# Letting GpSimd take some of VectorE's exponent shifts, in half tiles, in a planned transformer block

## The chip, the core and the metric

The kernel runs on one core of a Trainium2 chip. The engines that matter are TensorE (PE, matrix products), VectorE (DVE), ScalarE (ACT), GpSimd (POOL) and the DMA queue of SyncE (SP). Each engine works through its own list of instructions in order and waits on semaphores for the others. The metric is the device time of one execution in microseconds; the median of the runs shown is 819.32 us.

## The reference, cut to what matters

One transformer block with 2048 tokens of width 512, 32 heads of size 16, and a hidden width of 1376. Six modulation vectors come from a conditioning vector `c`.

```
h = layernorm(x) * (1 + ca) + sa
q, k, v = split(h @ wqkv)                   # 32 heads of 16
p = softmax(q k^T * 16**-0.5)               # 2048 x 2048 for each head
x = x + ga * ((p v) @ wo)
h = layernorm(x) * (1 + cb) + sb
x = x + gb * (gelu(h @ w1 + b1) @ w2 + b2)
```

The exponentials dominate: 32 heads of 2048 by 2048, over 134 million of them.

## The kernel before, in words

**Tiles.** Scores are held transposed, keys on partitions. Queries are cut into 4 blocks of 512 and heads into 8 groups of four, which makes 32 quads, `quads` (block, group). A quad has 16 key tiles of 128, and each key tile has 4 rows, one a head: a score row is a 128x512 product (`qk`, L1019). Four heads lie in four 32-row strips of the array.

**Two ways to an exponential.** Most key tiles go to ScalarE: `do_qk` puts units of 3 and 2 score rows in turn into PSUM tiles `sA` and `sB`, and `do_exp` (L1071) makes `pA` and `pB` with one ACTIVATE each. Four key tiles of a quad (`DKT`, in the first quad one) go through VectorE instead. `do_d` puts one score row at a time into one of two spare PSUM banks (`aux`). `do_pass` (L1137) adds a bias, clamps at zero and writes the number as int16 into a row of the tile `t0` (128x4x512). These 16 bits, read as float16, are roughly the wanted power of two. Three further copies, each `t0` plus a constant `MJ[j]`, are the same power scaled down by a fraction of a power of two; `do_shift` (L1155 to L1162, the instruction on L1158) makes each of them as one 128x2048 int16 instruction on VectorE, into a tile `t16`. There are 125 such tiles, so 500 passes and 375 shifts. Each of the four versions is multiplied with its own scaled copy of the values and all are summed, so that the mean of four rough powers approximates the exponential.

**Value products.** `do_pv` (L1190) multiplies a key tile, or one of its four versions, with the values and sums into one bank `od` for the quad. `do_out` (L1242) copies the sum to `o_sb` and sends the row sums through DRAM and back for the reciprocals (L1264); GpSimd then multiplies (`OT`, L1272). When all quads of a block are done, its output projection, MLP and result follow as jobs among the next block's quads (`tail_jobs`); the last block's come at the end (`last_tail`). A second way through the computation for extreme inputs (`general_path`) is not taken here.

**What sets the order.** While the program is built, a small planner steps a clock by 0.02 us (`DT`). At each step it asks the engines in turn, ACT, DVE, PE, POOL, SP (L1441), and the first thing that an engine finds ready is issued and booked with a price: `V_PASS` and `V_SHIFT` 0.61 us, an exponential 1.34 (three rows) or 0.92 (two), a GpSimd product 1.2 or 1.3. `run` (L960) moves that engine's `free` time; a result is seen by others 0.1 us (`SEM`) after its end. The chip then runs each engine's list in the planned order, held together by semaphores alone, not by the plan's times.

VectorE's step (`dve_step`, L1399) takes, in this order: a quad's `o_sb` copy, a job, a pass if a score row is ready, a shift. With more than four shifts pending a shift goes ahead of a pass. `shift_ready` (L1149) asks for a pending shift and a free `t16` (4 buffers). `shifts` gets its three entries when the last pass of a tile is issued (`do_pass`). `d_items` holds the score rows that were issued and not passed yet, two at most; `d_ready` (L1095) also asks for a free one of 3 `t0` tiles. GpSimd's step (`pool_step`, L1418) knows jobs alone: the `OT` products, eight weight scalings (`scale_wo`, L405) and twelve residual sums (L688). If more than one score tile of a quad is unstarted when the stream of ScalarE's rows runs dry, `fill_stream` (L992) gives one to ScalarE. `do_fill` (L1224) puts products with zeros into gaps of TensorE.

Of the kernel before, what the change touches and what calls it, by code (L numbers as in the profile page):

```python
# [11 lines left out]
ALU = mybir.AluOpType  # L12
# [3 lines left out]
I16 = mybir.dt.int16  # L16
# [4 lines left out]
P = 128  # L21
# [29 lines left out]
PE_, ACT_, DVE_, POOL_, SP_ = range(5)  # L51
# [22 lines left out]
V_PASS = 0.61  # L74
V_SHIFT = 0.61
V_EVAC = 0.63
TRIP = 5.0


# [8 lines left out]
MJ = [int(round(-math.log2(w) * STEP)) for w in WJ]  # L88
# [5 lines left out]
def adaln_block(ctx: ExitStack, tc: tile.TileContext, A_x, A_wqkv, A_wo, B_x, B_w1, B_b1, B_w2, B_b2,  # L94
                c, w_mod, out):
    nc = tc.nc
# [46 lines left out]
    def later_loads():  # L143
# [6 lines left out]
        for b in range(2, NQB):  # L150
# [19 lines left out]
                            op0=ALU.mult, op1=ALU.add)  # L170
# [41 lines left out]
    def ln_stats(src, st, t, i):  # L212
        nc.vector.bn_stats(out=st[:, i, :], in_=src[:, t, :])
# [101 lines left out]
    def q_proj(ps, ch, b, js=range(NC)):  # L315
        for j in js:
            nc.tensor.matmul(out=ps, lhsT=W_q[:, j, ch * P:(ch + 1) * P], rhs=hT[:, j, b * 512:(b + 1) * 512],  # L317
                             start=(j == 0), stop=(j == NC - 1))

    def q_evac(ps, ch, b, both=True):  # L320
        t = qmp.tile([P, 2, 512], BF16, name="qm")
        for par in range(2):
            if par and not both:
                nc.scalar.mul(out=t[:, par, :], in_=ps, mul=qmask[:, par:par + 1])
            else:
                nc.vector.tensor_scalar(out=t[:, par, :], in0=ps, scalar1=qmask[:, par:par + 1], scalar2=None,
                                        op0=ALU.mult)
        qm[(b, ch)] = t

    def v_proj(ps, kt, js=range(NC)):  # L330
        for j in js:
            nc.tensor.matmul(out=ps, lhsT=hT[:, j, kt * P:(kt + 1) * P], rhs=W_v[:, j, :],
                             start=(j == 0), stop=(j == NC - 1))

    def v_evac(ps, kt, eng="dve"):
        src = ps.rearrange("p (h d) -> p h d", d=16)
        dst = VE[:, kt, 0:H * HS].rearrange("p (h e) -> p h e", e=HS)[:, :, 0:16]
        if eng == "act":
            nc.scalar.copy(out=dst, in_=src)
        else:  # L340
            nc.vector.tensor_copy(out=dst, in_=src)
# [81 lines left out]
    tp = att.enter_context(tc.tile_pool(name="tp", bufs=T_BUFS))  # L423
# [16 lines left out]
    def job(at, rows, needs=(), label=None, hold=-1):  # L440
        jobs.append(Job(at, rows, needs, label, hold))
# [24 lines left out]

    def proj_job(at, mm, evac, needs, label, eng=DVE_, dur=V_EVAC):
        def f(part):
            def h(j):
                if part == 0:  # L470
                    j.ps = j.alloc()
                mm(j.ps, (0, 1) if part == 0 else (2, 3))
            return h

        def g(j):
            evac(j.ps)
        job(at, [(PE_, 2 * MM, f(0)), (PE_, 2 * MM, f(1)), (eng, dur, g)], needs, label, 2)

    def v_job(at, kt):
        eng = V_ENG[kt]  # L480
        proj_job(at, lambda ps, js: v_proj(ps, kt, js), lambda ps: v_evac(ps, kt, eng), [("h", kt // 4)], ("v", kt),
                 ACT_ if eng == "act" else DVE_, 0.5 if eng == "act" else V_EVAC)

# [3 lines left out]
    def q_job(at, ch, b, needs=()):  # L487
        proj_job(at, lambda ps, js: q_proj(ps, ch, b, js), lambda ps: q_evac(ps, ch, b), [("h", b), *needs],
                 ("q", ch, b), dur=2 * V_EVAC + 0.1)

# [12 lines left out]
    for b in range(1, NQB):  # L503
        at = 0.25 * (b - 1)
        def stats(j, b=b, t=0):
            if b > 1 and t == 0:
                st_of[b] = pron.tile([P, 12, 6], FP32, name="st1")
            ln_stats(xb[b], st_of[b], t, t)
        job(at - 0.16, [(DVE_, V_EVAC, lambda j, b=b, t=t, f=stats: f(j, b, t)) for t in range(ST1 if b == 1 else 0, 4)],
            [("n", b - 1)] if b > 1 else [], ("st", b))  # L510
# [81 lines left out]
    def tail_jobs(b):  # L592
# [15 lines left out]
        def oproj(tt):  # L608
            def f(part):
                def g(j):  # L610
                    if part == 0:
                        j.ps = j.alloc()
                        nc.tensor.matmul(out=j.ps, lhsT=ident, rhs=T["xr"][:, tt, :], start=True, stop=False)
                    for t in (2 * part, 2 * part + 1):
                        nc.tensor.matmul(out=j.ps, lhsT=OT[(b, t)][:, tt * P:(tt + 1) * P], rhs=W_o_pad[:, t, :],  # L615
                                         start=False, stop=(t == 7))
                return g
# [4 lines left out]
            def stats(j):  # L622
                ln_stats(T["x1"], T["st"], tt, tt)
            job(p0 + 0.5 + 0.25 * tt, [(PE_, (2 + (i == 0)) * MM, f(i)) for i in range(4)]
                + [(DVE_, V_EVAC, res), (DVE_, V_EVAC, stats)],
                [("begin", b)] + [("wo", t) for t in range(8)] + [("ot", b, t) for t in range(8)] + ([("o", b, tt - 2)] if tt > 1 else []),
# [20 lines left out]
        def up_(fc):  # L647
            def f(part):
                def h(j):
                    if part == 0:  # L650
                        j.ps = j.alloc()
                    for c in (2 * part, 2 * part + 1):
                        nc.tensor.matmul(out=j.ps, lhsT=late["W_1"][:, c, fc * P:(fc + 1) * P],  # L653
                                         rhs=T["h2"][:, c, :], start=(c == 0), stop=(c == NC - 1))
                return h

            def g(j):
                nc.vector.tensor_scalar(out=T["u"][:, fc, :], in0=j.ps, scalar1=late["b1c"][:, fc:fc + 1],  # L658
                                        scalar2=None, op0=ALU.add)
            job(p0 + 2.3 + 0.2 * fc, [(PE_, 2 * MM, f(0)), (PE_, 2 * MM, f(1)), (DVE_, V_EVAC + 0.05, g)],  # L660
                [("h2", b, c) for c in range(NC)], ("u", b, fc), 2)
# [283 lines left out]
    clock = 0.0  # L945
    free = [0.0, 0.0, 1.0, 0.0, 0.0]
# [6 lines left out]
    def seen_by(t):  # L953
        return t is not None and t + SEM <= clock
# [5 lines left out]
    def run(eng, dur, lat=0.08):  # L960

        free[eng] = clock + dur
        return clock + dur + lat

    def pe_run(dur, m):
        end = run(PE_, dur + (SWITCH if m != mode[0] else 0.0), PE_LAT)
        mode[0] = m
        pe_log.append((clock, dur))
        return end
# [119 lines left out]
    t0, t0_seq, t0_done = {}, [], {}  # L1089
    t_of, t_ready, shifts = {}, {}, deque()  # L1090
    t16_seq, pv_end = [], {}
    d_items, d_read = deque(), []
# [53 lines left out]

    d_prog = [0.0]

    def shift_ready():  # L1149
        if not shifts:  # L1150
            return False
        n = len(t16_seq)
        return n < T_BUFS or seen_by(pv_end.get(t16_seq[n - T_BUFS]))

    def do_shift():  # L1155
        qi, kt, j = shifts.popleft()
        t16 = tp.tile([P, 4, 512], I16, name="t16")
        nc.vector.tensor_scalar(out=t16, in0=t0[(qi, kt)], scalar1=float(MJ[j]), scalar2=None, op0=ALU.add)  # L1158
        end = run(DVE_, V_SHIFT)
        t16_seq.append((qi, kt, j))  # L1160
        t_of[(qi, kt, j)] = t16
        t_ready[(qi, kt, j)] = end  # L1162
        t0_done[((qi, kt), j)] = end


    od = {}
# [75 lines left out]
    def do_out(qi):  # L1242
# [27 lines left out]
        def mult(j):  # L1270
# [4 lines left out]
        needs = [("o", b - 1, tt) for tt in range(4)] if b and t else []  # L1275
        lab[("d", qi)] = end + TRIP
        jobs.insert(0, Job(-1.0, [(DVE_, 0.26, back), (SP_, TRIP, lambda j: None), (POOL_, 1.3, mult)],
                           [("d", qi), *needs], ("ot", b, t)))
# [12 lines left out]
    def start_ok(o, eng):  # L1291
        if o.at > progress() or o.rows[0][0] != eng or not all(has(x) for x in o.needs):
            return False
        if o.hold >= 0:
            if progress() > EARLY and any(a.hold >= 0 and a.i <= a.hold for a in active):
                return False
            return any(seen_by(t) for t in bank_rel)
        return True

    def job_for(eng):  # L1300

        best = None
        for o in active:
            if o.rows[o.i][0] == eng:
                same = o.i and o.rows[o.i - 1][0] == eng
                if (o.same if same else o.other) <= clock + 1e-6 and (best is None or o.at < best.at):
                    best = o
        for o in jobs[:24]:
            if best is not None and best.at <= o.at:
                break  # L1310
            if start_ok(o, eng):
                return o
        return best

    def do_job(o, eng):
        if o in jobs:
            jobs.remove(o)
            active.append(o)
            if o.hold >= 0:
                o.bank = next(i for i in range(len(banks)) if seen_by(bank_rel[i]))  # L1320
                bank_rel[o.bank] = INF
        e, dur, fn = o.rows[o.i]
        fn(o)
        if eng == PE_:
            end = pe_run(dur, "full")
            dur = free[PE_] - clock
        else:
            end = run(eng, dur)
        row_end(o, eng, dur, end)
# [86 lines left out]
        return False  # L1416

    def pool_step():  # L1418
        o = job_for(POOL_)
        if o is None:  # L1420
            return False
        do_job(o, POOL_)
        return True

    def sp_step():
        o = job_for(SP_)
# [60 lines left out]
```

## Time and profile before

| | |
|---|---|
| timed runs | 817.38, 819.32, 819.41 us; median 819.32 |
| the profiled execution | 815.8 us, span 814.0 us |
| granted TensorE clock | 0.996 |
| PE, DVE, ACT, POOL busy | 771.9, 723.8, 756.2, 71.2 us |
| passes (L1137) | 500, mean 682 ns |
| shifts (L1158) | 375, mean 715 ns, 629 to 1766 |
| exponentials pA, pB (L1071) | 310 and 309, mean 1513 and 1089 ns |
| GpSimd's OT products (L1272) | 31, mean 1394 ns |

How to read the profile: the page gives each engine's busy time, then the span in 40 slices with the busy tenths of each. A group's line is: source line, engine, operation, tiles written and read, shape, count, then busy us and mean ns of one, then the engine's idle time just before these instructions and what ended most of it. A timeline's line is: start and duration in us, engine, source line, operation, tiles, shape and count, and in brackets the idle time before; neighbours of a kind may be merged into one line. A windows line gives, for a stretch, the busy time of PE, PEld (weight loads), DVE, ACT and POOL with their counts, then the granted clock, the DMA share and GB/s. Durations of queued instructions overlap a little, so that the spacing of starts is the better measure of what one costs.

### The profile page before, as it was taken

The numbers are of one execution on the slowest core, as the hardware profiler recorded it, in microseconds if no ns is written. First come the engines' busy times: TensorE is split into PE (matmuls) and PEld (weight loads), VectorE is DVE, ScalarE is ACT, GpSimd is POOL, SyncE is SP. The second block draws the span as 40 slices with busy tenths as digits, with TensorE's granted clock in tenths as the row PEclk, the third lists the DMA queues.
The fourth block names the chain that finished last, engine by engine and source line by source line (L and its number), as shares of the span: only waits on it lengthen the run. The fifth ranks groups of instructions, "written<-read, shape, count | busy, mean of one in ns | idle before, by whom it ended". The sixth has DMA issues, their size and how long they took to land.

```text
span 814.0 us, 18164 instructions
## 1 busy us (share of the span) xinstructions
PE 771.9 (95%) x7404; PEld 237.5 (29%) x7470; DVE 723.8 (89%) x1306; ACT 756.2 (93%) x681; POOL 71.2 (9%) x62
## 2 busy tenths in 40 slices
PE   7999999989999999999999999999999999999997
PEld 3432222322223222222222322222222222222254
DVE  7879989999998998998998999988998999889663
ACT  4898999989998999999999999999999999999962
POOL 0000000024000000101100000011100000011100
PEclk9999999999999999999999999999999999999999
DMA  8100000104100000001100000010100000010100
GB/s 269 68 1 16 15 16 15 42 16 140 41 15 16 15 17 2 14 23 29 48 16 16 16 10 8 14 29 21 48 15 16 15 3 15 15 28 23 48 2 29
DMA packets 30426, 24.49 MB, mean 30 GB/s; under 512 B 13473, under 2 KB 24194, under 8 KB 30338
## 3 DMA queue, kind: packets, MB, share of 16 engines
q1 hardware_dynamic: 29650, 22.49, 9.6%
q8 instruction: 60, 0.98, 0.5%
q10 hardware_dynamic: 688, 0.79, 0.3%
q14 instruction: 28, 0.23, 0.1%
HBM read 20.65 MB, written 2.61 MB: 29 GB/s over the span
## 4 chain that ended last, share of the span: by engine, by line
PE 46%; ACT 24%; DVE 17%; issue 10%; DMA 2%; SPq 0%; POOL 0%; ACTq 0%; DVEq 0%; POOLq 0%
PE od L1214 14%; ACT pA L1071 14%; ACT pB L1071 9%; DVE t L1137 7%; PE sA L1019 6%; PE sB L1019 6%; DVE t L1158 6%; PE aux L1019 4%; PE aux L678 3%; PE od L1235 2%; PE aux L615 2%; PE aux L653 2%; PE aux L303 1%; PE fb L805 1%; PE aux L317 1%
## 5 line engine op out<-in xcount | busy, mean ns | idle before, releaser
L1071 ACT ACTIVATE pA<-sA 128x1536 bf16<-128x1536 f32 x310 | 469.1, 1513 | 16.3 <-PE od L1214 7.2
L1137 DVE TENSOR_SCALAR t<-aux 128x512 int16<-128x512 f32 x500 | 328.8, 682 | 30.6 <-PE aux L1019 29.2
L1071 ACT ACTIVATE pB<-sB 128x1024 bf16<-128x1024 f32 x309 | 336.4, 1089 | 6.3 <-PE od L1214 3.9
L1158 DVE TENSOR_SCALAR t<-t 128x2048 int16<-128x2048 int16 x375 | 260.1, 715 | 2.6 <-PE od L1214 1.4
L1019 PE MATMUL aux<-qm,kT 32*128 32x512 bf16 x500 | 177.5, 380 | 6.2 <-DVE t L1137 3.4
L1019 PEld LDWEIGHTS <-kT 32*128 32x128 bf16 x2048 | 75.9, 91 | 266.9 <-issue 262.6
L1214 PE MATMUL od<-pA,VE 128*32 128x512 bf16 x930 | 141.7, 385 | 0.6 <-DVE o_sb L1253 0.5
L1214 PE MATMUL od<-t,VV 128*32 128x512 f16 x1500 | 139.6, 385 | 1.5 <-DVE t L1158 1.2
L1214 PE MATMUL od<-pB,VE 128*32 128x512 bf16 x618 | 140.7, 385 | 0.1
L1019 PE MATMUL sA<-qm,kT 32*128 32x512 bf16 x930 | 123.0, 384 | 10.5 <-ACT pA L1071 4.7
L1019 PE MATMUL sB<-qm,kT 32*128 32x512 bf16 x618 | 121.1, 384 | 5.3 <-ACT pB L1071 2.4
L1272 POOL TENSOR_TENSOR OT<-o_sb,rb 128x512 bf16<-128x512 f32 x31 | 43.2, 1394 | 559.3 <-DMA rb<-d 288.4
L1214 PEld LDWEIGHTS <-VE 128*32 128x32 bf16 x2048 | 50.3, 94 | 95.9 <-issue 83.2
L1235 PE MATMUL od<-hT,zeros 128*32 128x512 bf16 x844 | 76.0, 385 | 0.0
L1214 PEld LDWEIGHTS <-VV 128*32 128x32 bf16 x1500 | 39.7, 95 | 58.8 <-issue 50.2
L1214 PE MATMUL od<-t,VE 128*32 128x512 f16 x500 | 49.5, 384 | 2.7 <-DVE o_sb L1253 2.7
L678 PE MATMUL aux<-W,uG 128*128 128x512 bf16 x120 | 35.5, 383 | 1.6 <-issue 1.6
L653 PE MATMUL aux<-h2T,W 128*128 128x512 bf16 x113 | 35.6, 384 | 0.5 <-issue 0.3
L1235 PEld LDWEIGHTS <-zeros 128*32 128x32 bf16 x872 | 21.8, 95 | 36.1 <-issue 30.6
L658 DVE TENSOR_SCALAR uG<-aux,b1c 128x512 bf16<-128x512 f32 x33 | 24.4, 741 | 4.8 <-PE aux L653 4.8
L615 PE MATMUL aux<-W_o_pad,OT 128*128 128x512 bf16 x88 | 25.6, 382 | 0.7 <-issue 0.5
L688 POOL TENSOR_TENSOR ob<-tmp,xr 128x512 bf16<-128x512 f32 x12 | 15.7, 1305 | 115.1 <-DVE tmp L684 115.1
(156 smaller groups left out, 430.9 us busy)
## 6 DMA issues: line engine op xcount, KB each, us to landing
rb<-d SPq DMA_DIRECT2D x124, 64.0 KB
W_m<-in_w_mod_dram SPq DMA_DIRECT2D x2, 1024.0 KB
xr<-in_A_x_dram SPq DMA_DIRECT2D x4, 512.0 KB
out_dram<-ob SPq DMA_DIRECT2D x15, 128.0 KB
xb<-in_A_x_dram SPq DMA_DIRECT2D x3, 512.0 KB
W<-in_B_w_dram SPq DMA_DIRECT2D x1, 1376.0 KB
W<-in_B_w_dram SPq DMA_DIRECT2D x1, 1280.0 KB
W_m<-in_w_mod_dram SPq DMA_DIRECT2D x1, 512.0 KB
```

Source lines behind the costliest of these rows:

```text
L615: nc.tensor.matmul(out=j.ps, lhsT=OT[(b, t)][:, tt * P:(tt + 1) * P], rhs=W_o_pad[:, t, :], start=False, stop=(t == 7))
L653: nc.tensor.matmul(out=j.ps, lhsT=late["W_1"][:, c, fc * P:(fc + 1) * P], rhs=T["h2"][:, c, :], start=(c == 0), stop=(c == NC - 1))
L658: nc.vector.tensor_scalar(out=T["u"][:, fc, :], in0=j.ps, scalar1=late["b1c"][:, fc:fc + 1], scalar2=None, op0=ALU.add)
L678: nc.tensor.matmul(out=j.ps, lhsT=T["u"][:, fc, tt * P:(tt + 1) * P], rhs=late["W_2"][:, fc, :], start=False, stop=(fc == NFC - 1))
L688: nc.gpsimd.tensor_tensor(out=o, in0=j.tmp, in1=T["x1"][:, tt, :], op=ALU.add)
L1019: nc.tensor.matmul(out=dst, lhsT=kT[32 * r:32 * r + 32, ch, kt * P:(kt + 1) * P], rhs=qm[(b, ch)][32 * r:32 * r + 32, par, :], start=True, ...
L1071: nc.scalar.activation(out=pt[:, 0:n, :], in_=st[:, 0:n, :], func=ACT.Exp, scale=math.log(2.0) / STEP)
L1137: nc.vector.tensor_scalar(out=t0[(qi, kt)][:, r, :], in0=sd, scalar1=T_BIAS, scalar2=0.0, op0=ALU.add, op1=ALU.max)
L1158: nc.vector.tensor_scalar(out=t16, in0=t0[(qi, kt)], scalar1=float(MJ[j]), scalar2=None, op0=ALU.add)
L1214: nc.tensor.matmul(out=od[qi][32 * r:32 * r + 32, :], lhsT=w, rhs=src, start=first, stop=last_)
L1235: nc.tensor.matmul(out=dst[32 * r:32 * r + 32, :], lhsT=zeros, rhs=hT[:, r, 0:512], start=bank is not None, stop=bank is not None)
L1272: nc.gpsimd.tensor_tensor(out=OT[(b, t)], in0=o, in1=j.rb, op=ALU.mult)
```

## The change

GpSimd may take a shift too, as two instructions over half of the tile each (two rows, 128x1024). A variable `port` in the planner holds the time up to which a shift, of either engine, is booked; no shift of either engine begins before that. It is not set by GpSimd's other work. GpSimd begins a shift when it has no job, a shift is ready, and at least one score row waits in `d_items`; the second half goes ahead of jobs, as soon as the booked time allows. A half is priced at 1.2 us. The shift's result counts as ready after the second half.

```diff
+P_SHIFT = 1.2
...
+    port = [0.0]
+    pool_cur = []
+
+    def shift_ready(eng=DVE_):
+        if not shifts or clock < port[0]:
             return False
...
         end = run(DVE_, V_SHIFT)
+        port[0] = free[DVE_]
...
+    def pool_shift():
+        if pool_cur:
+            key, t16 = pool_cur.pop()
+            part = 1
+        else:
+            key, part = shifts.popleft(), 0
+            t16 = tp.tile([P, 4, 512], I16, name="t16")
+            t16_seq.append(key)
+        qi, kt, j = key
+        nc.gpsimd.tensor_scalar(out=t16[:, 2 * part:2 * part + 2, :], in0=t0[(qi, kt)][:, 2 * part:2 * part + 2, :],
+                                scalar1=float(MJ[j]), scalar2=None, op0=ALU.add)
+        end = run(POOL_, P_SHIFT)
+        port[0] = free[POOL_]
+        if part == 0:
+            pool_cur.append((key, t16))
+        else:
+            t_of[key] = t16
+            t_ready[key] = end
+            t0_done[((qi, kt), j)] = end
...
     def pool_step():
+        if not pool_cur:
+            o = job_for(POOL_)
+            if o is not None:
+                do_job(o, POOL_)
+                return True
+        if pool_cur and clock >= port[0] or shift_ready(POOL_) and pool_may():
+            pool_shift()
+            return True
+        return False
+
+    def pool_may():
+
+        return len(d_items) >= 1
```

More of the change, by code (lines that the diff above doesn't have):

```diff
@@ L1147, in adaln_block @@
     d_prog = [0.0]
-    def shift_ready():
-        if not shifts:
+    port = [0.0]
+    pool_cur = []
+    def shift_ready(eng=DVE_):
+        if not shifts or clock < port[0]:
             return False
@@ L1418, in pool_step @@
     def pool_step():
[L1419 to L1423, printed above, removed]
+        if not pool_cur:
[9 more added lines that the diff above has]
+        return len(d_items) >= 1
     def sp_step():
```

## The prediction

> **What bounds the kernel now.** I read the page's busy lines first, to see which engines can matter.
>
> ```profile
> PE 771.9 (95%) x7404; PEld 237.5 (29%) x7470; DVE 723.8 (89%) x1306; ACT 756.2 (93%) x681; POOL 71.2 (9%) x62
> ## 2 busy tenths in 40 slices
> PE   7999999989999999999999999999999999999997
> ...
> DVE  7879989999998998998998999988998999889663
> ACT  4898999989998999999999999999999999999962
> ```
>
> Three engines are nearly full from about 60 to 770 us, and GpSimd is nearly empty. The groups say what each does:
>
> ```profile
> L1071 ACT ACTIVATE pA<-sA 128x1536 bf16<-128x1536 f32 x310 | 469.1, 1513 | 16.3 <-PE od L1214 7.2
> L1137 DVE TENSOR_SCALAR t<-aux 128x512 int16<-128x512 f32 x500 | 328.8, 682 | 30.6 <-PE aux L1019 29.2
> L1071 ACT ACTIVATE pB<-sB 128x1024 bf16<-128x1024 f32 x309 | 336.4, 1089 | 6.3 <-PE od L1214 3.9
> L1158 DVE TENSOR_SCALAR t<-t 128x2048 int16<-128x2048 int16 x375 | 260.1, 715 | 2.6 <-PE od L1214 1.4
> ```
>
> TensorE's 95% contains 844 filler multiplies (L1235). So the question is where ScalarE loses time, because its exponentials can't be shortened by this change. Its busy share hides that: a queued instruction is recorded as lasting longer than its pitch. I therefore took starts from ScalarE's timeline. Undisturbed, pA to pB is 1.33 us and pB to the next pA 0.91, so 2.24 a pair. Everything above that between the first and the last exponential adds up to **35.3 us**: 9.3 before 100 us, 1.1 from 100 to 150, 12.7 from 150 to 300, and 12.2 after that. No gain can pass this. The windows show why 150 to 300 is worst:
>
> ```profile
> 150.00:200.00 50.00, 46.84 (x508) 13.51 (x510) 48.45 (x83) 46.91 (x42) 11.46 (x13) 0.97 0.23 70
> 200.00:250.00 50.00, 47.39 (x452) 13.53 (x453) 46.88 (x75) 45.58 (x40) 5.63 (x4) 1.00 0.08 23
> 700.00:750.00 50.00, 48.05 (x468) 14.04 (x468) 43.50 (x72) 50.00 (x45) 6.74 (x5) 1.00 0.08 21
> ```
>
> The columns are PE, PEld, DVE, ACT, POOL. VectorE is at 48.45 of 50 where ScalarE falls to 46.91; late in the run VectorE has air (43.50) and ScalarE is full.
>
> One more view decides this case, the timeline around a GpSimd multiply:
>
> ```profile
> 583.21 1.27 POOL L1272 TENSOR_TENSOR OT<-o_sb,rb 128x512 bf16<-128x512 f32 x1 [11.10 <-DMA rb<-d]
> ...
> 583.34 1.69 DVE L1158 TENSOR_SCALAR t<-t 128x2048 int16<-128x2048 int16 x1
> ...
> 586.15 1.23 ACT L1071 ACTIVATE pB<-sB 128x1024 bf16<-128x1024 f32 x1
> ...
> 587.45 1.45 ACT L1071 ACTIVATE pA<-sA 128x1536 bf16<-128x1536 f32 x1
> ```
>
> A shift that starts under a GpSimd instruction doesn't slow down in proportion: it ends 0.55 us after GpSimd does (584.48 and 585.03), in 1.69 us where an undisturbed one takes 0.685. The passes (L1137, from PSUM) under the same multiplies keep their 0.68. The reverse holds too: that multiply, 1.27 us alone, lasts up to 1.84 behind a shift. So shifts and GpSimd exclude each other and passes do not. Here the delay of 1.0 us cost ScalarE 0.4: 1.30 from pB to pA in place of 0.91. I found eight shifts stretched by about 0.8 to 1.1 us and put ScalarE's next gaps beside them: 2.9 us after the two at 170 to 172, 1.9 after the two at 200 to 202, then 0.3, 0.9, 0.4, 0.6 after those at 213, 282, 583 and 606. That is 7.0 us, 0.9 a collision, 0.5 where VectorE has some air. Shorter ones (513, 650) cost nothing.
>
> **The change, part by part.**
>
> *How many shifts move.* GpSimd may take a shift when no shift runs and a score tile waits in a bank. In the trace a tile's three shifts are pending for 5.25 us on average (start of its last pass to start of its third shift); in 117 of 125 tiles there is a moment in that time when no shift runs and a score row has been issued but not passed. A moved shift holds the port 2.4 us by the plan's price, so two a tile is the ceiling. I take a little over one: 140 of 375, which is 280 half instructions.
>
> *Removed from VectorE.* 140 shifts at their start-to-start pitch of 0.60 (two in 1.28-1.29 us) are 84 us, 724 down to 640.
>
> *Added to GpSimd.* The trace has no one-input integer instruction on it. From below: a memset with no input, 0.205 us for 128x128 and 0.525 for 128x512, so 0.83 ns an element and 0.95 us for 1024. From above: the two-input product, 1.16 us undisturbed for 512, twice that for 1024, 2.3. The middle is about 1.6. I take 1.2, the plan's price, because the plan's other prices sit on the rows: 0.61 for a pitch of 0.60, 1.2 for a product of 1.16, 1.3 for one of 1.27, and one input lies nearer to the memset. GpSimd gains 280 x 1.2 = 336 us, 71 to 407, half the span, beside other work.
>
> The Trainium skill bears on this price from both sides: GPSIMD Engine Reference, "Engine selection", calls one-input work on GpSimd roughly line rate, while its section "Elementwise — side-by-side cycle accounting" gives about 1.8 cycles an element as the best of a tight loop. At the 1.2 GHz of that page, estimates are 0.85 us a half by the one, the forecast's side, and 1.5 by the other, where the first rival begins.
>
> *Queue order on GpSimd.* A half stands behind multiplies that wait for a DMA (L1272, 288 us of idle before it). The first ones start 4.9 to 5.2 us after the reciprocal; the plan allows 5.0 plus semaphores. Little is held up; at nothing. A multiply may wait for two halves, 2.4 us; the output projection that needs it comes quads later, so this costs nothing unless it is a group's last.
>
> *The wait that is new.* TensorE runs in order, so a value product waiting for a late t16 holds every score behind it. Today TensorE waits for shifts 1.2 us in all. From a shift's end to the first product on it the median is 1.3 us, but 120 of 375 have under 0.8. I charge 0.5 us.
>
> *The sum.*
> - Of the 7.0 us after collisions: fewer shifts are left (235 of 375) and they queue less, so half goes, -3.5.
> - Of the other 6.7 us lost from 150 to 300, where VectorE is full: half, -3.3.
> - Of the other 11.2 after 300, where it isn't: a tenth, -1.1.
> - Before 100 us shifts are few: 0.
> - New collisions: the order keeps halves and shifts apart on paper, but engines only keep to it through their semaphores. I allow 6 of 280 halves that stop a shift by 0.8 us or more, 0.5 each, +3.0.
> - Late t16: +0.5.
>
> Together -4.4 us. The profiled execution took 815.8 us (span 814.0 and 1.8 around it), so 811.4; the three timed runs have their median 3.5 higher, and from 819.3 I forecast **814.9 us**. A difference of 0.3% (2.5 us) is about what a measurement of this kernel can tell from no change.
>
> **The rivals.**
>
> *A, a half is dearer than its price* (slower). Every moved shift ends late by twice the excess, and the next shift on VectorE, placed right behind it, is stopped that long with all passes behind it. The relief is 0.60 a shift, so it decides from 1.2 + 0.30 = 1.5 us a half. At the middle, 1.58, 140 x (0.76 - 0.60) = 22 us, on a VectorE that is full in part of the run: some 17, or 836. At 2.2 it would be 140 x 1.4, near 200, or over 1000. For it: the product's 2.3 ns an element. Against: the memset's 0.83.
>
> *B, the exclusion costs more than the plan sees* (slower) though a half takes 1.2. The plan books a GpSimd half from the moment it places it; on the chip it starts when the last pass has written t0 and the shift in front has ended. In 69 tiles the chance falls inside the last pass, up to 0.69 us too early. If that shifts half of these so that the next shift is stopped for 0.8 us, at 0.5 each for 40, that is +20, less the gains of 7.9: +12, 831. For it: the rows at 583. Against: the passes run on, and VectorE has 84 us of relief. The Trainium skill says the same in Perfetto Trace Analysis, "Optimizing Scalar/DVE Operations": because the two share a port, moving work between them might not help.
>
> *C, nothing comes of it.* ScalarE is full after 300 us, and the gaps before are TensorE's, or GpSimd seldom finds a shift free. 819.
>
> **How the numbers follow.** Forecast 0.40, A 0.19, B 0.24, C 0.17. The forecast's own range is 806 (both losses from 150 to 300 and those after collisions gone, 13.7) to 817. The upper bound of the price lies far out in A; two in ten are left out by stopping at 840, which takes in B and the mild half of A. Faster by over 0.3%: the forecast less its weak end, 0.38. Within: C and that weak end, 0.19. Slower: A and B, 0.43.
>
> **What would show it.** Right: GpSimd halves near 1.2 us, some 280 of them; VectorE's busy time down by 60 to 90 us; few shifts over 1.4 us; ScalarE's gaps from 150 to 300 halved. A: halves of 1.5 us or more, and TensorE waiting for GpSimd by tens of us. B: halves of 1.2, but dozens of shifts over 1.4 us. C: all moved, ScalarE's gaps as before. I would also be wrong if score tiles of the exponent path went over to ScalarE (fewer than 500 passes).

## The result, and the profile after

The changed kernel takes **1147.69 us** (median of its runs, 1140.24 to 1155.53), the one before 818.35 in the same runs: **1.402 times as long, 95% interval 1.397 to 1.408**. The forecast of 814.9 and its whole range, up to 840, are missed by far. The profiled execution took 1143.97 us, with a span of 1141.9 in place of 814.0 and a granted clock of 0.825 in place of 0.996.

First the busy lines of the page, with the slices of GpSimd and of the granted clock:

```profile
PE 946.8 (83%) x7418; PEld 246.5 (22%) x7486; DVE 722.3 (63%) x1160; ACT 781.3 (68%) x681; POOL 905.7 (79%) x354
...
POOL 0069999889997986988997889957995977989820
PEclk9995886978769689798878888899679676688899
```

GpSimd went from 9% to 79%, and through most slices it stands at 7 to 9 tenths. The three engines that were nearly full are now at 63 to 83%. The windows view from 80 to 1080 us says it in microseconds (PE, PEld, DVE, ACT, POOL, clock, DMA share, GB/s):

```profile
80.00:1080.00 1000.00, 823.45 (x6461) 196.84 (x6516) 631.04 (x934) 688.10 (x573) 880.12 (x339) 0.80 0.06 16
```

GpSimd works for 880 of 1000 us: it is now the fullest engine. The groups show with what, and who waits:

```profile
L1181 POOL TENSOR_SCALAR t<-t 128x1024 int16<-128x1024 int16 x292 | 839.8, 2900 | 144.8 <-DVE t L1139 91.0
L1073 ACT ACTIVATE pA<-sA 128x1536 bf16<-128x1536 f32 x310 | 452.2, 1459 | 185.5 <-PE sA L1021 98.1
L1139 DVE TENSOR_SCALAR t<-aux 128x512 int16<-128x512 f32 x500 | 332.3, 684 | 302.1 <-PE aux L1021 249.5
L1241 PE MATMUL od<-t,VV 128*32 128x512 f16 x1500 | 205.7, 448 | 155.6 <-POOL t L1181 154.8
L1164 DVE TENSOR_SCALAR t<-t 128x2048 int16<-128x2048 int16 x229 | 224.4, 1004 | 16.7 <-PE od L1241 11.9
```

292 halves, so 146 shifts, were moved, and each half takes 2.9 us, not 1.2. TensorE idles 154.8 us in front of the products on their results; VectorE and ScalarE wait for TensorE's scores in turn (249.5 and 98.1). The 229 shifts left on VectorE grew from 715 to 1004 ns, so that all shifts together fell by 35.7 us only (260.1 to 224.4). Its busy time stayed at 722.3 all the same, because the records of a less crowded engine overlap less (55.1 us of overlap in place of 87.0). One wait of TensorE for a half in the timeline:

```profile
319.64 11.27 POOL L1181 TENSOR_SCALAR t<-t 128x1024 int16<-128x1024 int16 x4
...
323.58 0.64 PE L1241 MATMUL od<-t,VV 128*32 128x512 f16 x2
...
325.50 0.61 PE L1241 MATMUL od<-t,VV 128*32 128x512 f16 x2 [1.28 <-POOL t L1181]
...
327.17 1.45 ACT L1073 ACTIVATE pA<-sA 128x1536 bf16<-128x1536 f32 x1 [2.80 <-PE sA L1021]
```

Four halves run back to back, one every 2.8 us. TensorE has issued the products on the first half of a t16 and stands before those on the second; the scores behind them come late, and ScalarE idles 2.80 us. Added up as in the prediction, ScalarE's gaps went from 35.3 to 363.2 us: 327.9 more. That is the whole difference of the spans (327.9), so nothing outside the stretch of the exponentials changed.

The theory with which I went into the runs: the price of a half is the cause, and GpSimd, overbooked by the plan, bounds the run. The rivals: the exclusion of the two engines would cost as much whatever a half takes; and the granted clock (0.825, with 448 ns for a value product of a shift in place of 385) is a cause of its own.

### The profile page after: what moved, and what is told of

It is laid out like the page before. It is cut to its first block, busy times and chain, and to the rows that moved or that the text cites. A ratio compares the mean times of both kernels' runs of the same rounds, so it can differ in the third digit from the quotient of the medians.

```text
span 1141.9 us, 18545 instructions
## 1 busy us (share of the span) xinstructions
PE 946.8 (83%) x7418; PEld 246.5 (22%) x7486; DVE 722.3 (63%) x1160; ACT 781.3 (68%) x681; POOL 905.7 (79%) x354
## 5 line engine op out<-in xcount | busy, mean ns | idle before, releaser
L1181 POOL TENSOR_SCALAR t<-t 128x1024 int16<-128x1024 int16 x292 | 839.8, 2900 | 144.8 <-DVE t L1139 91.0
L1073 ACT ACTIVATE pA<-sA 128x1536 bf16<-128x1536 f32 x310 | 452.2, 1459 | 185.5 <-PE sA L1021 98.1
L1139 DVE TENSOR_SCALAR t<-aux 128x512 int16<-128x512 f32 x500 | 332.3, 684 | 302.1 <-PE aux L1021 249.5
L1073 ACT ACTIVATE pB<-sB 128x1024 bf16<-128x1024 f32 x309 | 318.7, 1031 | 139.5 <-PE aux L1021 91.4
L1241 PE MATMUL od<-t,VV 128*32 128x512 f16 x1500 | 205.7, 448 | 155.6 <-POOL t L1181 154.8
L1164 DVE TENSOR_SCALAR t<-t 128x2048 int16<-128x2048 int16 x229 | 224.4, 1004 | 16.7 <-PE od L1241 11.9
L1021 PE MATMUL aux<-qm,kT 32*128 32x512 bf16 x500 | 203.1, 450 | 9.0 <-DVE t L1139 7.9
L1241 PE MATMUL od<-pA,VE 128*32 128x512 bf16 x930 | 172.3, 443 | 0.8 <-DVE o_sb L1280 0.5
L1241 PE MATMUL od<-pB,VE 128*32 128x512 bf16 x618 | 165.8, 446 | 0.1
L1021 PE MATMUL sA<-qm,kT 32*128 32x512 bf16 x930 | 147.9, 442 | 8.8 <-ACT pA L1073 3.0
L1021 PE MATMUL sB<-qm,kT 32*128 32x512 bf16 x618 | 141.0, 441 | 3.9 <-issue 1.1
L1280 DVE COPY o_sb<-od 128x512 f32<-128x512 f32 x32 | 21.9, 684 | 16.4 <-PE od L1241 16.3
```

The source lines that it names most:

```text
L1021: nc.tensor.matmul(out=dst, lhsT=kT[32 * r:32 * r + 32, ch, kt * P:(kt + 1) * P], rhs=qm[(b, ch)][32 * r:32 * r + 32, par, :], start=True, ...
L1073: nc.scalar.activation(out=pt[:, 0:n, :], in_=st[:, 0:n, :], func=ACT.Exp, scale=math.log(2.0) / STEP)
L1139: nc.vector.tensor_scalar(out=t0[(qi, kt)][:, r, :], in0=sd, scalar1=T_BIAS, scalar2=0.0, op0=ALU.add, op1=ALU.max)
L1181: nc.gpsimd.tensor_scalar(out=t16[:, 2 * part:2 * part + 2, :], in0=t0[(qi, kt)][:, 2 * part:2 * part + 2, :], scalar1=float(MJ[j]), scala ...
L1241: nc.tensor.matmul(out=od[qi][32 * r:32 * r + 32, :], lhsT=w, rhs=src, start=first, stop=last_)
L1280: nc.vector.tensor_copy(out=o, in_=od[qi])
```

## The experiments

**What a half costs by itself (e1_alone).** To the kernel before, right at GpSimd's start, are added the disputed instruction in several sizes and its alternatives, on a tile not yet in use; the computation is unchanged.

```diff
+    def add(o, i, n):
+        for r in range(n):
+            nc.gpsimd.tensor_scalar(out=o(md[r % 2]), in0=i(ms), scalar1=256.0, scalar2=None, op0=ALU.add)
+    add(lambda t: t[:, 0:2, :], lambda t: t[:, 0:2, :], 4)      # int16 128x1024
...
+        nc.gpsimd.tensor_tensor(out=md[r % 2][:, 0:2, :].rearrange("p a b -> p (a b)").bitcast(I32),     # int32 128x512
...
+        nc.gpsimd.tensor_copy(out=md[r % 2][:, 0:2, :], in_=ms[:, 0:2, :])
```

> The kernel before, with rows of GpSimd instructions added in its first 50 us, when GpSimd has nothing else to do and VectorE makes no shift; nothing waits for them and the computation is unchanged. In this order: int16 add of a constant on 128x1024 (four), 128x512 (three), 128x400 (three), the same add on bfloat16 128x1024 (three), an int32 add of a broadcast constant on 128x256 (three) and on 128x512 (three, which are the same bytes as 1024 int16), an int16 copy 128x1024 (two). Theory (the half is dear by itself): the int16 halves follow each other every 2.7 us, 128x512 takes half of that, 128x400 about 1.1. Rival (a half is cheap and only VectorE's shifts stretch it): 1.2 us or less with no shift beside it.

The groups of GpSimd in the first 40 us of this kernel, kept apart by shape:

```profile
L173 POOL TENSOR_SCALAR W_o_pad<-W_o_pad 128x1024 int16<-128x1024 int16 x4 | 11.0, 2777 | 0.1
L173 POOL TENSOR_SCALAR W_o_pad<-W_o_pad 128x1024 bf16<-128x1024 bf16 x3 | 8.3, 2780 | 0.1
L173 POOL TENSOR_SCALAR W_o_pad<-W_o_pad 128x512 int16<-128x512 int16 x3 | 4.4, 1482 | 0.0
...
L182 POOL TENSOR_TENSOR W_o_pad<-W_o_pad,mk 128x512 int32<-128x512 int32 x3 | 3.0, 1037 | 0.1
L186 POOL COPY W_o_pad<-W_o_pad 128x1024 int16<-128x1024 int16 x2 | 2.0, 1046 | 0.1
```

The half takes 2.78 us with no shift of VectorE beside it (2.73 from start to start), above even the upper end of the prediction (2.3). It isn't the integers: bf16 costs the same. 128x512 takes 1.48, so an element costs 2.5 ns and the start little. A copy of the same tile takes 1.05. The Trainium skill (GPSIMD Engine Reference, "Engine selection") calls one-input elementwise work on GpSimd roughly line rate; by these rows that holds for the copy and not for this add, and the measurement decides. The same bits come from an int32 addition of the constant in both halves of a word, 512 words a half, in 1.04 us: a tool for the next experiments. (The kernel as a whole took 826.19 us in its one run; the added instructions stand ahead of all of GpSimd's work.)

**The same plan and order with a half of 1.0 us (e5_packed).** Every instruction stays in its place; only the half becomes the int32 addition.

```diff
-        nc.gpsimd.tensor_scalar(out=t16[:, 2 * part:2 * part + 2, :], in0=t0[(qi, kt)][:, 2 * part:2 * part + 2, :],
-                                scalar1=float(MJ[j]), scalar2=None, op0=ALU.add)
+        nc.gpsimd.tensor_tensor(out=words(t16, part), in0=words(t0[(qi, kt)], part),      # int32 views
+                                in1=mj_w[:, j:j + 1].to_broadcast([P, 512]), op=ALU.add)   # mj_w: MJ[j] * 65537
```

> The changed kernel in its own order, with the same plan and price (1.2), but each half made by another GpSimd instruction that gives the same bits: an int32 add of a constant that holds the shift twice, on 512 int32 in place of 1024 int16, 1.00 us a piece in e1_alone in place of 2.73. Theory (the wrong price makes the loss: results come 3 us late and TensorE waits in order): the waits of TensorE for GpSimd nearly vanish and the time falls to 810 to 850 us. Rival (a moved shift costs by the exclusion and by its longer way, whatever it takes): over 900 us.

853.0 us, 1.042 times the kernel before (1.039 to 1.046). Of the 329 us, 295 went with the price. It is 3 us above the 850 that I had allowed, and what is left still misses the forecast, though this half (1.13 us on average in this kernel) is cheaper than the 1.2 that it assumed. TensorE's waits for GpSimd, from the waits view of this kernel (total, times, longest), and GpSimd's timeline at the longest:

```profile
PE od L1247 <- POOL t L1187: 10.0, 3, 8.5
```

```profile
200.08 0.19 POOL L581 CAST b1c<-b_bf 128x11 f32<-128x11 bf16 x1 [11.09 <-DMA b_bf<-in_B_b_dram]
200.23 3.03 POOL L1187 TENSOR_TENSOR t<-t,mj_w 128x512 int32<-128x512 int32 x3
```

A small cast in GpSimd's queue waits 11.09 us for a DMA, and the halves wait behind it. TensorE stands 8.55 us.

**That cast out of the way (e8_cast).** As e5_packed, with the cast issued as a job later.

```diff
-        nc.gpsimd.tensor_copy(out=b1c, in_=b1_bf)
+    job(8.2, [(POOL_, 0.2, lambda j: nc.gpsimd.tensor_copy(out=late["b1c"], in_=late["b1_bf"]))], ["late"], "b1c")
```

> As e5_packed, with one thing taken out of GpSimd's queue: the cast of the MLP's bias vector, which there waits 11 us for its DMA (189 to 200 us) with shifts queued behind it, is issued some 1.7 quads later, when its data has long come. Theory (one stretch of 9.3 us of ScalarE's gaps in e5_packed is this queue, and the half clock after it): 853 falls by 9 to 16 us, to 837 to 844. Rival (another cause that only falls together with it): no change, 850 to 856.

848.59 us, 1.037 (1.032 to 1.042). TensorE's waits for GpSimd fall from 10.0 to 4.7 us, but the time by 4.4 only, less than expected, with intervals that touch. In place of the long gap of ScalarE stand small ones between 180 and 206 us and one of 4.05 us that ends at 210.8: now the `OT` product at 203.43 stands at the head of GpSimd's queue, after 7.09 us of waiting for its DMA, with halves behind it, and TensorE waits 2.66 us for one of them.

**The plan knows the price (e3_priced).** The int16 half again, and the planner's price set to what it takes.

```diff
-P_SHIFT = 1.2
+P_SHIFT = 2.75
```

> The changed kernel with the plan's price of a half at 2.75 us in place of 1.2, nothing else. Theory (the loss comes from a price that is wrong, so that TensorE meets value products whose shift isn't there): the plan moves fewer shifts, TensorE hardly waits for GpSimd, and nearly all of the 329 us is gone: 815 to 860 us. Rival (the exclusion of the two engines costs it, whatever the plan knows): GpSimd still holds the shifts up, over 950 us.

922.54 us, 1.127 (1.124 to 1.129). The plan moves 97 shifts where it moved 146, TensorE waits for GpSimd for 3.3 us in place of 154.8, and the time is still far above the 860 that I allowed. The waits view of ScalarE in this kernel:

```profile
ACT pA L1073 <- PE od L1241: 68.4, 14, 11.2
ACT pB L1073 <- PE od L1241: 31.5, 8, 7.4
```

ScalarE now waits for free p buffers. A tile's shifts, excluding each other by `port`, come 5.5 us apart where GpSimd has one, and the quad's products stand in the planned order behind them: it looks as if the wait has moved from the chip's queues into the plan. The plan itself saw such gaps, for it put 2112 filler products into `od` where the kernel before has 844. A rival stands beside this: by the 0.55 us a half of the next experiment, exclusion alone would be 194 x 0.55 = 107 us, as much as the whole loss of 103. No run separates the two. An honest price alone does not make the change pay.

**The exclusion alone (e4_side, e7_side_packed).** To the kernel before, with all its 375 shifts on VectorE, are added 150 halves that read and write unused slices of another tile (`hT`), so that no result of the kernel needs theirs. In e4 they are the int16 addition, in e7 the int32 one, in the same places.

```diff
+        if shifts and len(d_items) >= 1 and has(("q", 3, 1)):
+            nc.gpsimd.tensor_scalar(out=hT[:, 2:4, 512:1024].bitcast(I16), in0=hT[:, 0:2, 512:1024].bitcast(I16),
+                                    scalar1=256.0, scalar2=None, op0=ALU.add)      # e7: the int32 addition
+            run(POOL_, 2.75)
+            return True
```

> The kernel before, with VectorE making all shifts as before, and with int16 halves of the same size on GpSimd from about 200 us on, whenever a shift is pending, a score row waits and GpSimd is free by the plan; they write to a tile that is not needed any more, and nobody waits for them. It leaves nothing out and shows the price of the exclusion by itself. Theory (late results cost the time, not the exclusion): up to 4% over the kernel before, 850 us at most. Rival (exclusion): shifts of 1.4 us in large numbers and well over 900 us.

> As e4_side (VectorE makes all shifts, GpSimd halves beside it that nobody waits for, at the same places of the plan, one per 2.75 us at most), but with the int32 instruction of 1.0 us in place of the int16 one of 2.73. It separates how the exclusion is priced. If it goes by the time that GpSimd holds the port: e4_side's 82 us for 150 pieces shrink with the length, to about 30, 850 us. If it goes by the piece (one VectorE shift stopped by each): near 900 us again.

e4: 901.46 us, 1.098 (1.094 to 1.102). e7: 869.36, 1.064 (1.058 to 1.069). The shifts on VectorE, first in e4 and then in e7:

```profile
L1158 DVE TENSOR_SCALAR t<-t 128x2048 int16<-128x2048 int16 x375 | 341.5, 931 | 3.5 <-PE od L1214 2.2
```

```profile
L1158 DVE TENSOR_SCALAR t<-t 128x2048 int16<-128x2048 int16 x375 | 305.3, 835 | 2.8 <-PE od L1214 1.5
```

715 ns became 931 and 835. VectorE's busy time grew by 86.5 and 47.5 us, the spans of the same executions by 92.8 and 47.8, the medians by 82 and 50: on an engine that was nearly full, exclusion is paid about one for one, some 0.55 us for an int16 half and 0.33 for an int32 one. Neither is quite the exclusion alone. In e4 TensorE is at half clock for 92.4 us in place of 8.9. In e7 the filler products, which read other slices of `hT`, do wait for the halves, as they don't in e4:

```profile
PE od L1235 <- POOL hT L1424: 8.6, 14, 1.0
```

e4 is over the 850 that its theory allowed at most and short of its rival's "well over 900"; e7 lies between its two. A half that is 2.7 times as long stops VectorE only 1.8 times as much (86.5 and 47.5): the price lies between one by the time held and one by the number of pieces.

**A finer price (e6_packed_105), and few shifts (e11_few).** e6 is e5_packed with the price at 1.03. e11 is e8_cast with a price of 1.1 and a stricter rule: GpSimd may begin only with both score rows waiting, so that only 26 shifts move.

```diff
-        return len(d_items) >= 1
+        return len(d_items) >= 2        # e11
```

> As e5_packed, with the plan's price at 1.03 us, what the half takes. The plan then moves more shifts and keeps VectorE out of the port for less long. Theory: like e5_packed or a little better, 800 to 845 us; rival: no better than e5_packed, since every further moved shift adds to the exclusion.

> As e8_cast, but GpSimd may begin a shift only when both spare banks hold a score row (two in d_items, not one) and the price is 1.1 us: 26 shifts move, in place of 146. Theory (each moved shift costs by exclusion and queue, and ScalarE gives nothing back): near the kernel before, 815 to 830 us, not under it by over 0.3%. Rival (a small number moved relieves VectorE where it is full, the rest does the harm): 805 to 815.

e6: 855.07, 1.046 (1.042 to 1.050), no better than e5. e11: 843.81, 1.031 (1.026 to 1.035), a miss for both sides: a sixth of the shifts moved, and most of e8's loss stays. What one collision can do, from e11's timeline, GpSimd first, then VectorE and ScalarE:

```profile
459.15 2.48 POOL L1187 TENSOR_TENSOR t<-t,mj_w 128x512 int32<-128x512 int32 x2 [7.35 <-DVE t L1145]
...
459.37 2.82 DVE L1170 TENSOR_SCALAR t<-t 128x2048 int16<-128x2048 int16 x2
...
462.10 0.53 DVE L306 TENSOR_SCALAR h2T<-aux,modc 128x512 bf16<-128x512 bf16 x1
...
462.69 0.58 PE L1027 MATMUL aux<-qm,kT 32*128 32x512 bf16 x1 [2.16 <-DVE h2T L306]
...
465.82 1.02 ACT L1079 ACTIVATE pB<-sB 128x1024 bf16<-128x1024 f32 x1 [0.95 <-PE aux L1027]
```

Two halves meet two shifts, which take 2.82 us instead of 1.29. Behind them in VectorE's queue stands the copy that empties a spare bank (h2T), so TensorE waits 2.16 us; and from 462.0 to 472.2 us the granted clock is 0.50. ScalarE works 5.76 of those 10.2 us. The prediction had priced a collision at 0.5. That the clock makes the difference here is read from this trace alone. e11 also has another planned order than e8, and what adds up to its 24 us in all was not settled.

**A half that keeps VectorE out for next to nothing (e12_thin).** As e8_cast, same plan and order, but a half makes only 64 of its 512 columns, and the value products read those eight times over. This leaves out seven eighths of each moved shift.

```diff
+        nc.gpsimd.tensor_tensor(out=t16[:, 2 * part:2 * part + 2, 0:64].bitcast(I32), ...)
...
+                if (qi, kt, j) in by_pool:
+                    src = t_of[(qi, kt, j)][:, r, 0:64].bitcast(F16).unsqueeze(1).to_broadcast([P, 8, 64])
```

> As e8_cast, in the same order, but each GpSimd half makes only the first 64 of a row's 512 columns, and the value product repeats these 64 columns eight times (it leaves out seven eighths of a moved shift's work; TensorE's and VectorE's instructions keep their shapes and places). This makes GpSimd nearly free, 0.2 us a half, so that neither exclusion nor lateness is left, while VectorE is relieved of the 146 shifts. Theory (ScalarE is the bound, so even a free GpSimd gains next to nothing): 808 to 822 us. Rival 1 (the relief of VectorE is worth something that the exclusion hides): under 808. Rival 2 (the new order itself, not the exclusion, makes what is left in e8_cast): 835 or more.

823.02 us, 1.005 (1.003 to 1.007), 1 us above what my theory allowed. The busy lines of this kernel, and its halves:

```profile
PE 782.2 (96%) x7486; PEld 236.8 (29%) x7486; DVE 653.9 (80%) x1160; ACT 756.4 (92%) x681; POOL 164.7 (20%) x357
...
L1188 POOL TENSOR_TENSOR t<-t,mj_w 128x64 int32<-128x64 int32 x292 | 98.7, 357 | 394.6 <-DVE t L1145 214.0
```

VectorE is relieved by 69.9 us, about what the forecast hoped for, and on balance nothing comes of it: ScalarE's gaps are 38.3 us against 35.3, its busy time is unchanged, and the kernel is no faster. But the gaps are not the same ones. From 150 to 300 us there are 11.5 us of them against 12.7, and 5.2 of the 11.5 are a single hole:

```profile
198.12 1.26 POOL L1310 TENSOR_TENSOR OT<-o_sb,rb 128x512 bf16<-128x512 f32 x1 [10.87 <-DMA rb<-d]
...
201.57 0.54 POOL L1188 TENSOR_TENSOR t<-t,mj_w 128x64 int32<-128x64 int32 x2
...
201.91 0.86 PE L1252 MATMUL od<-t,VV 128*32 128x512 f16 x4 [4.51 <-POOL t L1188]
```

GpSimd waits 10.87 us for the DMA of an `OT` product, the halves of a shift stand behind it, and TensorE waits 4.51 us for them. Without this hole 6.3 us are left in that stretch, half of before. The relief of VectorE did close gaps there; GpSimd's queue opened another.

**TensorE kept at work while it waits (e10_warm, e13_warm4).** To the changed kernel are added products with zeros ahead of each value product that reads a GpSimd shift, 8 in e10 and 32 in e13, so that TensorE doesn't idle in its waits and its clock holds.

```diff
+        if (qi, kt, j) in by_pool and not first:
+            for r in [0, 1, 2, 3] * 8:          # e10: * 2
+                nc.tensor.matmul(out=od[qi][32 * r:32 * r + 32, :], lhsT=zeros, rhs=hT[:, r, 0:512], start=False, stop=False)
```

> The changed kernel with its int16 halves and its order, plus eight filler products with zeros (1.7 us at full clock, not booked by the plan) ahead of each value product on a shift that GpSimd made: more work for TensorE, 146 x 1.7 = 250 us of it at most, placed where TensorE would wait. Theory (waits and, through them, the half clock make the loss, so filling the waits keeps the clock): granted clock from 0.825 to over 0.92 and the time no longer than the changed kernel's 1148, rather 1080 to 1140. Rival (the clock is a side effect, TensorE's load is the bound): the time rises by 100 us or more.

> As e10_warm, with four times the fillers, 32 ahead of each value product on a GpSimd shift. Four fillers run side by side in the array's strips, so e10_warm added 145 x 0.43 = 62 us and not 250 as written there; this one adds 250. Theory (the half clock is part of the loss): granted clock near 0.97, the time under e10_warm's 1134, 1060 to 1120. Rival (TensorE's load is the bound, the clock only follows): 1200 or more.

e10: 1134.07, 1.387 (1.377 to 1.396), within the time that the theory named, but its fillers were too few to tell: four run side by side in the strips, so they added some 62 us of work and not the 250 expected, and the clock rose to 0.89 only. e13: 1146.79, 1.402 (1.398 to 1.406). That is neither the theory's 1120 at most nor the rival's 1200. The busy line and the clock of e13:

```profile
PE 1057.3 (93%) x12158; PEld 355.6 (31%) x12158; DVE 717.8 (63%) x1160; ACT 774.8 (68%) x681; POOL 902.2 (79%) x354
...
PEclk9999999979899999999999999999999999899999
```

The clock is back at 0.982, the time at half clock falls from 402.6 us to 43, and the kernel takes as long as without it. GpSimd's busy time is the same (902.2 and 905.7). So the low clock was a companion of the waits and at most a small part of the loss. One reservation: the fillers are work themselves, TensorE is at 93% with them, and they could hide a gain of the clock by their own cost; e10, with a quarter of them, bounds what showed of such a gain at 13.6 us.

## Why the prediction was wrong, point by point

The same order of instructions with ever cheaper halves gives the parts of the loss:

| kernel | a half | median us | less |
|---|---|---|---|
| after | 2.9 us | 1147.7 | |
| e5_packed | 1.13 us | 853.0 | 294.7 the price |
| e8_cast | 1.13 us, cast moved | 848.6 | 4.4 the cast |
| e12_thin | 0.36 us | 823.0 | 25.6 the rest of a half's time |
| before | none | 818.8 | 4.2 the order, and what thin halves still cost |

- **The number of shifts** was right, by a guess of a little over one a tile: 140 forecast, 146 moved, and 500 passes as before.
- **The price of a half is the step that failed.** I set the upper bound by the two-input product (2.3 us) and went below it to 1.2, because one input "lies nearer to the memset" and because the plan's other prices were right. No row had this operation, and both arguments were guesses about its kind: alone it takes 2.73 to 2.78 us. The step that would have warned me even so is a sum that I did not make: 280 x 2.3 + 71 is 715 us of GpSimd, nearly the whole span, at my own upper bound. With 292 x 2.76 + 71 it is 877, so GpSimd had to become the bound. In the same order, a half of 1.13 us took 294.7 of the 329 us back.
- **Rival A** named the cause, and its formula with the measured price gives 140 x (2 x 1.56 - 0.60) = 353 us where 329 were measured. Its sign came true as well, TensorE waiting for GpSimd by tens of us. The mechanism of its formula was not the one seen: that had VectorE stopped for twice the excess, but VectorE is 37% idle. The near agreement is luck as far as these runs show, and no proof of the formula. Its chance was too small because I weighed prices near 1.6 and treated those above 2.2 as a tail.
- **84 us off VectorE.** None came in the changed kernel (723.8 to 722.3): the shifts that stayed were stretched, and only 35.7 us of shifts went. With halves of 1.13 us 35.5 came, with the thin ones 69.9.
- **The gains of 3.5, 3.3 and 1.1.** They came in no kernel's time. e12_thin, which gives VectorE nearly all of its relief, says where they went. Some 6 of these 7.9 us were to come between 150 and 300 us, where I took VectorE, at 48.45 and 46.88 of 50, to be what limits ScalarE. With VectorE at 43.35 from 150 to 200 us and 37.65 from 200 to 250, ScalarE's gaps of the whole stretch fell from 12.7 to 6.3 us beside the one hole of 5.2. That agrees with the reading, in one profiled execution; the hole comes from the term for GpSimd's queue. Before 100 us and after 300 the gaps grew by 1.9 us each, and no run says why.
- **New collisions, 6 of them, 0.5 each.** 51 of the 229 shifts took over 1.4 us and 108 over 0.9. At the price assumed, e5_packed and e8_cast still lose some 30 us, and e12 shows that 25.6 of them hang on the time a half takes, with TensorE's own waits for GpSimd equal (4.7 and 4.5). That fits rival B's mechanism, the exclusion, at 25.6 where B had 20 before its gains. The time at half clock falls between the two kernels as well, from 39.9 to 18.3 us, and no run separates its share.
- **Queue order on GpSimd, at nothing.** I looked at the first multiplies that wait for the reciprocals and overlooked the cast, which waits for a load: 9.3 us of ScalarE's gaps in e5. Moving it brought 4.4, and a multiply took its place at the head of the queue (4.05 us in e8, 5.2 in e12). Both waits stood in the trace of before, in the two lines under this list, where no shift stood behind them. The multiply there starts 13.0 us after its reciprocal; the plan allows 5.0, and the first ones take 4.9 to 5.2.
- **A late t16, 0.5 us.** 154.8 in the changed kernel, 10.0 and 4.7 with cheap halves. This too was mostly a matter of price.

The two waits in GpSimd's queue, in the kernel before:

```profile
193.22 0.53 POOL L573 CAST b1c<-b_bf 128x11 f32<-128x11 bf16 x1 [12.52 <-DMA b_bf<-in_B_b_dram]
...
197.60 1.27 POOL L1272 TENSOR_TENSOR OT<-o_sb,rb 128x512 bf16<-128x512 f32 x1 [1.16 <-DMA rb<-d]
```

No kernel here beat the one before.

## What to carry to other kernels

Before work is moved to another engine, add up that engine's whole time at the upper end of every price you do not know: if it fills the span there, the price must be measured before anything else is worth working out, and a plan's own price is no measurement. Then read that engine's queue for its longest waits, not its usual ones, since all that is moved stands behind them; a nearly free GpSimd took 70 us off VectorE here and gained nothing on balance, in part for this. Where two engines exclude each other, a moved instruction costs both, and a full one pays about one for one.

## What the runs showed of the hardware

The int16 half lets VectorE in once in its middle. In the trace of the changed kernel, 104 halves begin with no shift running and have a shift begin under them. Where the first such shift begins in the half's first 0.9 us, it ends 1.58 us after the half's start (34 of 34). Where it begins between 0.93 and 1.7 us, it runs in an undisturbed 0.68 (28 of 29), and from about 1.25 us on the half itself grows, to 3.25 in place of 2.76 at most behind a single shift. A later one mostly ends 0.55 us after the half (32 of 39). The int32 half holds on throughout: in e7, 85 of the 91 shifts that begin under one end 0.55 us after its end. The Trainium skill (SBUF — State Buffer, "Who interferes with whom") gives the pair of ports that the two engines share to whichever starts first, for the whole instruction; the int32 rows agree, the int16 ones don't, and it may be that this half is carried out as two pieces, which no run here shows. Small VectorE instructions with two inputs are stopped as well: in e11 one of 128x4 took 0.92 us under a GpSimd half, in place of 0.16.
